# Output weight with 32 rows a partition, in an adaLN decode block with cached attention

## The chip, the cores and the metric

The kernel runs on one core of a Trainium2 chip. The metric is the device time of one execution in microseconds. Five engines work side by side: TensorE (PE) multiplies matrices, VectorE (DVE), ScalarE (ACT) and GpSimd (POOL) do the rest, and SyncE (SP) issues nearly all DMAs. Each core has 16 DMA engines, which move data between the off-chip memory and the on-chip memory of 128 partitions.

## The reference

One decode step (one new token a row) of a block with adaptive layer norm, batch of 4, width D = 512, 32 heads of 128, a cache of 4096 keys and values, and an MLP of width 1792. Everything is float32.

```python
mod = (_silu(c) @ w_mod).reshape(4, 6, 1, -1)
sa, ca, ga, sb, cb, gb = (mod[:, i] for i in range(6))
h = _layernorm(x) * (1 + ca) + sa
q = heads(h @ wq)                                   # 4, 32, 1, 128
p = softmax(einsum("bhqd,bhkd->bhqk", q, k_cache) * 128 ** -0.5)
o = einsum("bhqk,bhkd->bhqd", p, v_cache)           # 4, 32, 1, 128
x = x + ga * (rows(o) @ wo)                         # wo: 4096 x 512
h = _layernorm(x) * (1 + cb) + sb
x = x + gb * (_silu(h @ w1) @ w2)                   # w1: 512 x 1792, w2: 1792 x 512
```

The keys and values are 268 MB each, the weights wq and wo 8.4 MB each, w_mod 6.3 MB, w1 and w2 3.7 MB each.

## The kernel before, in words

A small planner (`Plan`) records every operation with the memory that it reads and writes, and from that derives the semaphore waits; each engine runs its operations in the order in which they are written. TensorE, VectorE and ScalarE run most tiles in a hardware loop.

Attention is cut into N = 32 tiles. A tile is one batch row b and four heads (group t of NT = 8), 8 MB of keys and 8 MB of values; a partition holds 128 keys of one head, a run of 64 KB. `tile(n)` multiplies the keys by the query, VectorE the first 48 of a partition's 128 and GpSimd the rest, sums over the head's width on VectorE, and makes the exponentials; `values(n)` multiplies them with the values on TensorE, normalizes, and writes four columns of `oz` (128 partitions are the head's width, a column is one head of one batch row). Tiles are counted with the batch row innermost: `t, b = divmod(n, B)`. `qw` holds the spread queries, which `qexpand(t)` writes for four batch rows at a time, `qview(n)` reads for a tile, and `qload(n)` copies into a PSUM bank.

Three big buffers of 64 KB a partition hold the stream: A and B take the keys of odd and even tiles, C takes the values. SyncE issues all loads in the order of the program through the one helper `dma` (L249 in the profile), and waits before each until its buffer is free: w_mod, wq, k0, v0, k1, and so on. After tile 30 B is free, and the output weight `wot` goes there, in four pieces behind the last values (`fetch(wot, wov, "o", 0, 4, 6, 7, 8)`). A is free after tile 31's keys; w1 (three pieces) and w2 (five pieces) go there.

In the output weight a partition holds, for each of the eight head groups t, four consecutive rows of wo, 8 KB:

```python
wov = wo.rearrange("(t p r) n -> p t r n", p=P, r=JJ)   # JJ = 4
```

`regroup()` brings the attention's output into that layout: 16 small TensorE matmuls against columns of the identity put `oz` into PSUM, two ScalarE copies bring it to `oz2`. Then 32 matmuls with 512 columns, spread over four column groups of the array, sum into `accw`. `fold` copies `accw` on ScalarE and adds its four groups with four matmuls into `accp`. From there on: gate and residual (`x1`), layer norm, transpose (`h2T`), w1's matmuls half by half (four pieces k of the contraction for the one half, its activation, then the other half), w2's matmuls as its pieces land (ten wide, a fold, then narrow ones straight into `pf`), gate and residual, and the store.

Matmuls are recorded by one helper line (L263), VectorE's two-operand operations by L272 and L276, ScalarE's by L295. A float32 matmul shows as two passes in the trace.

## Time and profile before

| | |
|---|---|
| median of 3 runs | 1319.59 us (1319.52 to 1319.98) |
| the profiled execution's own time | 1319.41 us |
| its span in the trace | 1318.0 us |
| bytes moved | 567.41 MB, 431 GB/s over the span |
| busy: TensorE, VectorE, ScalarE, GpSimd | 399.6, 884.4, 84.8, 710.9 us |
| SyncE's DMA queue (q1), share of 16 engines | 99.6% |

The span runs from the first instruction to the last; the profiled execution's time has 1.4 us more around it. Busy times of engines overlap. In rows of DMAs a packet is one piece of work of one DMA engine: here a contiguous run of data, or the 4 bytes with which an engine reports that its part of a DMA is complete. In the chain of waits each step leads back to what released it. In the timeline a row has the start, the duration, the engine, the line, the operation and its tiles (out<-in), the count, and in brackets the idle time before it with what ended it.

### The profile page before, as it was taken

To read this page: it belongs to the slowest core of one execution; us is meant where nothing else is said; L and a number is where in the kernel's file an instruction comes from. 1 tells how busy PE (TensorE), PEld (TensorE's weight loads), DVE (VectorE), ACT (ScalarE), POOL (GpSimd) and SP (SyncE) were. 2 spreads that over 40 slices of the span, in tenths; PEclk is the share of its full clock that TensorE was granted. 3 is DMA by queue.
4 is the path that set the end of the run, shared out by engine and by line. 5 is a ranking of instruction groups with operands and counts; after the bars stand their busy time and mean duration, and the time that the engine had idled before them with its cause. 6 is when DMAs were issued, how large, how long until landed. Compare 5 with 4: busy or idle time off the path is not lost.

```text
span 1318.0 us, 7633 instructions
## 1 busy us (share of the span) xinstructions
PE 399.6 (30%) x2748; PEld 115.5 (9%) x2748; DVE 884.4 (67%) x585; ACT 84.8 (6%) x288; POOL 710.9 (54%) x104
## 2 busy tenths in 40 slices
PE   2533222333321233322133332113333212333336
PEld 0100000000000000000000000000000000000012
DVE  1367876666876666687666678766667776666871
ACT  1200000000000000000000000000000000000001
POOL 0346665444666444566644456654446665445760
PEclk9766656666656666665666666566666556666668
DMA  9999999999999999999999999999999999999998
GB/s 414 437 424 440 432 432 442 422 440 438 424 442 432 432 440 422 442 438 424 440 428 438 438 424 442 436 426 440 426 438 440 424 442 430 432 440 422 430 425 357
DMA packets 12100, 567.41 MB, mean 431 GB/s; under 512 B 1292, under 2 KB 1340, under 8 KB 2108
## 3 DMA queue, kind: packets, MB, share of 16 engines
q1 hardware_dynamic: 12052, 567.29, 99.6%
q8 instruction: 4, 0.07, 0.0%
q14 instruction: 4, 0.03, 0.0%
q10 hardware_dynamic: 40, 0.02, 0.0%
HBM read 567.30 MB, written 0.01 MB: 430 GB/s over the span
## 4 chain that ended last, share of the span: by engine, by line
DMA 60%; DVE 24%; issue 9%; PE 5%; ACT 1%; SPq 1%; POOL 0%; DVEq 0%; ACTq 0%
DMA k<-in_A_k_cache_dram 55%; DVE sc L281 14%; DVE k L272 8%; PE ps L263 5%; DMA wqt<-in_A_wq_dram 3%; DMA w2t<-in_B_w_dram 2%; ACT sc L295 1%; SPq L249 1%; DVE pz L272 1%; DVE rt L516 1%; DVE nm L280 0%; POOL E L272 0%; DVEq L173 0%; DVE o L276 0%; ACT qs L295 0%
## 5 line engine op out<-in xcount | busy, mean ns | idle before, releaser
L272 POOL TENSOR_TENSOR k<-k,qw 128x3072 f32<-128x3072 f32 (+1 forms) x96 | 706.5, 7387 | 515.4 <-DMA k<-in_A_k_cache_dram 515.4
L263 PE MATMUL ps<-v,pz 128*16 128x512 f32 x2048 | 311.3, 751 | 844.4 <-DMA v<-in_A_v_cache_dram 804.3
L281 DVE TENSOR_REDUCE sc<-k 128x24 f32<-128x3072 f32 (+2 forms) x128 | 559.5, 4413 | 1.1
L272 DVE TENSOR_TENSOR k<-k,ps 128x6144 f32<-128x6144 f32 x32 | 209.7, 6555 | 227.5 <-DMA k<-in_A_k_cache_dram 227.3
L263 PEld LDWEIGHTS ps<-v,pz 128*16 128x16 f32 x2048 | 58.2, 114 | 1041.8 <-DMA v<-in_A_v_cache_dram 789.2
L295 ACT ACTIVATE sc<-sc,nm 128x80 f32<-128x80 f32 x64 | 22.3, 348 | 1005.4 <-DVE nm L280 1005.4
L276 DVE SCALAR_TENSOR_TENSOR o<-ps,fr,o 128x512 f32<-128x512 f32 x32 | 24.0, 751 | 53.0 <-PE ps L263 53.0
L272 DVE TENSOR_TENSOR pz<-sc,ps 128x320 f32<-128x320 f32 x64 | 27.0, 421 | 32.5 <-ACT sc L295 32.5
L263 PE MATMUL ps<-sel,o 128*128 128x4 f32 x256 | 33.8, 255 | 31.1 <-DVE o L276 31.1
L263 PEld LDWEIGHTS ps<-sel,o 128*128 128x128 f32 x256 | 31.0, 191 | 61.4 <-DVE o L276 61.4
L555 DVE RECIPROCAL fr<-ps 128x1 f32<-128x1 f32 x32 | 5.4, 168 | 42.5 <-PE ps L263 42.5
L272 POOL TENSOR_TENSOR E<-qs,sel 128x2048 f32<-128x2048 f32 x1 | 3.6, 3637 | 45.7 <-ACT qs L295 45.7
L295 ACT ACTIVATE o<-ps,fr 128x512 f32<-128x512 f32 x32 | 22.0, 687 | 60.7 <-DVE fr L276 60.7
L281 DVE TENSOR_REDUCE sc<-sc 128x1 f32<-128x80 f32 x64 | 14.1, 220 | 2.2
L516 DVE STREAM_TRANSPOSE rt<-sc 128x32 f32<-128x32 f32 x64 | 13.5, 211 | 2.2
L280 DVE TENSOR_REDUCE nm<-rt 128x1 f32<-128x32 f32 x64 | 11.9, 186 | 2.2
L272 DVE TENSOR_TENSOR x<-mod,ps 128x128 f32<-128x128 f32 x1 | 0.3, 286 | 18.4 <-PE ps L263 18.4
L272 DVE TENSOR_TENSOR E<-qs,sel 128x2048 f32<-128x2048 f32 x1 | 2.3, 2293 | 15.2 <-ACT qs L295 15.2
L263 PE MATMUL ps<-wqt,hT 128*32 128x512 f32 x64 | 9.0, 726 | 11.4 <-DMA wqt<-in_A_wq_dram 11.4
L263 PE MATMUL ps<-X,selp 128*128 128x2 f32 x64 | 12.3, 262 | 0.0
L263 PE MATMUL ps<-wmt,csT 128*32 128x256 f32 (+1 forms) x64 | 6.7, 590 | 18.2 <-DMA wmt<-in_w_mod_dram 18.2
L295 ACT ACTIVATION_READ_ACCUMULATOR sc<-sc,nm 128x1 f32 x64 | 11.9, 187 | 0.0
(70 smaller groups left out, 122.0 us busy)
## 6 DMA issues: line engine op xcount, KB each, us to landing
wmt<-in_w_mod_dram SPq DMA_DIRECT2D x1, 6144.0 KB, 17.3
k<-in_A_k_cache_dram SPq DMA_DIRECT2D x1, 5120.0 KB, 39.2
v<-in_A_v_cache_dram SPq DMA_DIRECT2D x1, 5120.0 KB, 24.8
wot<-in_A_wo_dram SPq DMA_DIRECT2D x1, 4096.0 KB, 37.2
k<-in_A_k_cache_dram SPq DMA_DIRECT2D x1, 3072.0 KB, 46.0
v<-in_A_v_cache_dram SPq DMA_DIRECT2D x1, 3072.0 KB, 27.6
wot<-in_A_wo_dram SPq DMA_DIRECT2D x1, 2048.0 KB, 41.7
wot<-in_A_wo_dram SPq DMA_DIRECT2D x2, 1024.0 KB, 43.9
```

Of the source, the lines that this page charges most:

```text
L249: return pl.op(eng, lambda: e.dma_start(dst, src), [], [dst], sem=s)
L263: lambda: nc.tensor.matmul(o, lhsT, rhs, start=start, stop=stop, skip_group_check=True),
L272: return q(lambda: e.tensor_tensor(o, a, b, op=op), [a, b], [o])
L276: return dve(lambda: V.scalar_tensor_tensor(o, a, s, b, op0=op0, op1=op1), reads, [o])
L280: return dve(lambda: V.tensor_reduce(o, a, axis=AX.X, op=op, negate=True), [a], [o])
L281: return dve(lambda: V.tensor_reduce(o, a, axis=AX.X, op=op), [a], [o])
L295: return act(lambda: A.activation(o, a, fn, **kw), reads, writes)
L516: dve(lambda: V.transpose(rt[:, h, :], a), [rm], [rt[:, h, :]])
L555: dve(lambda: V.reciprocal(fr[:, 0:1], fps[:, 0:1]), [fps[:, 0:1]], [fr[:, 0:1]])
```

## The change

The output weight is read with 32 consecutive rows of wo in each partition (64 KB of one head), in pieces of 16, 8, 4 and 4 rows. Its partitions are ordered by the quarter q of the head's width, then by head. Tiles are counted with the head group innermost, so that the columns of `oz` run through the 32 heads of a batch row; one VectorE transpose in blocks of 32 by 32 then puts `oz` into the weight's layout, and ScalarE and VectorE each spread half of it into `oz2`. The last four rows of the weight are multiplied narrowly, straight into `accp`, behind the fold. w1 comes in two pieces, and its last quarter is multiplied for both halves after the first three quarters of both.

```diff
+    QO = P // H
+    RO = Dh // QO
+    CUTO = (0, 16, 24, 28, 32)
...
-    oz = ozf[:, :].rearrange("p (t b i) -> p t b i", t=NT, b=B)
-    oz2 = sb("oz2", JJ, NT, W)
-    qw = sb("qw", NT, B * Dh)
+    oz2 = sb("oz2", RO, W)
+    qw = sb("qw", B, NT, Dh)
...
-    wot = big("B", "wot", NT, JJ, D)
+    wot = big("B", "wot", RO, D)
...
-    wov = wo.rearrange("(t p r) n -> p t r n", p=P, r=JJ)
+    wov = wo.rearrange("(h q r) n -> q h r n", q=QO, r=RO)
...
     def kload(n, *cuts):
-        t, b = divmod(n, B)
+        b, t = divmod(n, NT)
...
     def vload(n, *cuts):
-        t, b = divmod(n, B)
+        b, t = divmod(n, NT)
...
     def qexpand(t):
...
-        actv(qw[:, t, :], ps[:, :], AF.Copy)
+        actv(qw[:, :, t, :], ps[:, :].rearrange("p (b d) -> p b d", d=Dh), AF.Copy)
...
-    fetch(wot, wov, "o", 0, 4, 6, 7, 8)
+    for lo, hi in zip(CUTO, CUTO[1:]):
+        dma(wot[:, lo:hi, :], wov[:, :, lo:hi, :], f"o{lo}")

     def regroup():
-        for h in range(2):
-            ps = bank[(6, 0)[h]][:, :].rearrange("p (r t w) -> p r t w", r=2, t=NT)
-            for r in range(2):
-                for i in range(HP):
-                    mm(
-                        ps[W * i : W * (i + 1), r, :, :], ident[:, 2 * h + r : P : JJ],
-                        bc(oz[:, :, :, i], 3, R), True, True,
-                    )
-            actv(oz2[:, 2 * h : 2 * h + 2, :, :], ps, AF.Copy)
+        dve(lambda: V.transpose(ozt[:, :], ozf[:, :]), [ozf[:, :]], [ozt[:, :]])
+        src = bc(ozt[:, :].rearrange("p (b r) -> p b r", b=B), 3, R)
+        dst = oz2[:, :, :].rearrange("p r (b c) -> p b r c", b=B)
+        actv(dst[:, 0:2], src[:, 0:2], AF.Copy)
+        dve(lambda: V.tensor_copy(dst[:, 2:4], src[:, 2:4]), [src[:, 2:4]], [dst[:, 2:4]])
...
-    fetch(w1t, w1v, "a", 0, 2, 3, 4)
+    fetch(w1t, w1v, "a", 0, 3, 4)
     fetch(w2t, w2v, "b", 0, 7, 10, 12, 13, 14)
     regroup()
-    for i in range(NT * JJ):
-        g, (t, r) = i % G, divmod(i, JJ)
-        mm(accw[W * g : W * (g + 1), :], oz2[:, r, t, :], wot[:, t, r, :], i < G, i >= NT * JJ - G)
-    fold(accp, wide[0], accw, True, True)
+    RW = CUTO[-2]
+    for r in range(RW):
+        g = r % G
+        mm(accw[W * g : W * (g + 1), :], oz2[:, r, :], wot[:, r, :], r < G, r >= RW - G)
+    fold(accp, wide[0], accw, True, False)
+    for r in range(RW, RO):
+        for g in range(G):
+            mm(accp[W * g : W * (g + 1), :P], oz2[:, r, :], wot[:, r, g * P : (g + 1) * P], False, r == RO - 1)
...
-    for h, ph in ((0, bank[2]), (1, bank[6])):
...
+    halves = (bank[2], bank[6])
+    for k0, k1 in ((0, NK - 1), (NK - 1, NK)):
+        for h, ph in enumerate(halves):
+            pv_ = ph[:, :FH].rearrange("p (c i) -> p c i", i=NH)
+            for k in range(k0, k1):
+                for g in range(G):
+                    mm(
+                        pv_[W * g : W * (g + 1)], h2T[:, k, :], wv[:, k, g, :, NH * h : NH * (h + 1)],
+                        k == 0, k == NK - 1,
+                    )
+    for h, ph in enumerate(halves):
         silu2(hid[:, h, :], ph[:, :FH], hs[:, h, :])
         transposed(hidT[:, NH * h : NH * (h + 1), :], hid[:, h, :], NH)
```

## The prediction

> **What bounds the kernel now.** I read the page first: its slices and its table of DMA queues.

> ```profile
> span 1318.0 us, 7633 instructions
> ...
> DMA  9999999999999999999999999999999999999998
> DMA packets 12100, 567.41 MB, mean 431 GB/s; under 512 B 1292, under 2 KB 1340, under 8 KB 2108
> ...
> q1 hardware_dynamic: 12052, 567.29, 99.6%
> ...
> DMA 60%; DVE 24%; issue 9%; PE 5%; ACT 1%; SPq 1%; POOL 0%; DVEq 0%; ACTq 0%
> ```

> q1, SyncE's queue, keeps its 16 engines busy for 99.6% of the span. One engine thus moves 567.29 MB / (0.996 x 1318.0 us x 16) = 27.0 GB/s while busy. VectorE's 24% of the chain lies beside transfers; nothing but a change in the DMA work can move the time much. Second, the DMA view of the steady stretch, of the output weight, and the end of the chain of waits:

> ```profile
> DMA packets 7489, 436.22 MB, mean 434 GB/s; under 512 B 832, under 2 KB 832, under 8 KB 832
> ...
> DMA packets 801, 6.36 MB, mean 424 GB/s; under 512 B 64, under 2 KB 64, under 8 KB 64
> ...
> 1285.32 28.14 DMA w2t<-in_B_w_dram
> 1313.50 1.23 PE ps L263 x32
> 1314.78 0.47 PE ps L263 x8
> ```

> The first line is 205.27 to 1211.54 us (k and v alone: runs of 64 KB, 434 GB/s, 27.1 an engine), the second 1282 to 1297 us (output weight alone: runs of 8 KB, 424 GB/s). At the end the second MLP weight is what everyone waits for: after its last pieces only 1.7 us of matmuls, two small VectorE operations and the store are left. The order of arrival is v31, output weight, w1, w2, each 16 engines wide.

> **How a transfer is spread over the engines.** This decides the case. In the sums each DMA leaves small completion packets, so they can be counted. SyncE issues 80 loads (wm, wq, 33 k, 33 v, 4 wo, 3 w1, 5 w2). With three small DMAs (c, x, out) left over, 80 x 16 + 3 x 4 = 1292 is exactly the count of packets under 512 B above. So a load whose DRAM side starts with the 128 partitions posts 16 completions, and those three post 4. The three have in common that their DRAM side is written `(g) b d`, with an outer axis of 4. The store alone (1317.1 to 1317.5 us), and the load of c beside the first weight (5.9 to 7.7, then 7.7 to 9.5 us), show it:

> ```profile
> DMA packets 20, 0.01 MB, mean 21 GB/s; under 512 B 4, under 2 KB 20, under 8 KB 20
> ...
> q1 hardware_dynamic: 20, 0.01, 7.5%
> ...
> q1 hardware_dynamic: 16, 0.79, 100.9%
> q10 hardware_dynamic: 4, 0.00, 0.4%
> ...
> q1 hardware_dynamic: 16, 0.79, 100.8%
> q10 hardware_dynamic: 4, 0.00, 0.4%
> ```

> The store has 16 rows and 4 completions. c has 16 rows too, and in each stretch in which all 16 engines take one 48 KB packet of the weight (1.8 us), only 4 of c's rows go: four engines alternate between the queues, one row each a round, and twelve have no row of c at all. Completions and rows agree: an outer axis of 4 puts the whole DMA on 4 engines.

> [...]

> **The change, part by part.**

> *Output weight's load.* Before, `wov` is `p t r n`, outer axis 128, and 16 engines. After, it is `q h r n` with q = 4: sizes 4 and 128, four engines for all four pieces (8 KB loads with 4 and 16 are what the rows show; for 4 and 128 it is taken over). 8.389 MB / 4 = 2.097 MB an engine. The rate of an engine lies between 424 / 16 = 26.5 GB/s (8 KB runs) and 434 / 16 = 27.1 (64 KB runs). The new runs are 32, 16 and 8 KB, half of the bytes in 32, so I take 27.0, the page's mean: 77.7 us (77.4 to 79.1). What the load takes now is read from TensorE's waits, which end as each piece lands:

> ```profile
> 1287.54 3.64 PE L263 MATMUL ps<-wot,oz 128*32 128x512 f32 x32 [0.82 <-DMA wot<-in_A_wo_dram]
> 1292.41 1.92 PE L263 MATMUL ps<-wot,oz 128*32 128x512 f32 x16 [1.24 <-DMA wot<-in_A_wo_dram]
> 1294.90 1.07 PE L263 MATMUL ps<-wot,oz 128*32 128x512 f32 x8 [0.57 <-DMA wot<-in_A_wo_dram]
> 1297.39 1.73 PE L263 MATMUL ps<-wot,oz 128*32 128x512 f32 x8 [1.42 <-DMA wot<-in_A_wo_dram]
> ```

> The last three pieces (4.194 MB) take 1297.39 - 1287.54 = 9.85 us, 426 GB/s, so the whole takes 19.7 us. Difference 77.7 - 19.7 = +58.0 us (57.5 to 59.5). Nothing covers it. w1 and w2 go over 16 engines, and the four loaded ones must still carry their sixteenth of both behind the output weight, in order; the other twelve finish early and stand idle for about 58 us. The time from the last wo byte to the last w2 byte stays what it is, since those four engines still carry 0.459 MB each there (17 us at 27.0). The longer runs alone, on 16 engines, would be worth 19.7 us less 8.389 MB / 434 GB/s = 19.3: -0.4 us.

> *SyncE's queue.* The issues stop when an engine's ring is full:

> ```profile
> 1250.23 12.35 SPq L249 DMA_DIRECT2D wot<-in_A_wo_dram  x4
> ...
> 1280.31 11.45 SPq L249 DMA_DIRECT2D w2t<-in_B_w_dram  x5
> ...
> q1 hardware_dynamic: 9580, 546.28, 100.0%
> ```

> The last line is the DMA view from 0 to 1262.58 us, when wo's fourth issue ends: 9580 / 16 = 599 packets an engine are out. Issued are 68 loads of 9 (8 rows and a completion) and wo's 33 + 17 + 9 + 9: 680. So about 81 packets wait in each ring when an issue is let through. After, each wo piece puts 32 + 1 packets on four engines, 132 in all. The third and fourth issue, and w1 and w2 behind them in SyncE's order, are held until those rings drain to some 80. That holds back twelve empty engines, but not the four that set the end: with 40 to 80 packets waiting they don't run dry. Priced 0; upper bound a dry gap before the later three pieces and before w1, each as long as the store takes from issue to its first packet (1315.91 to 1317.2 us, 1.3): 4 x 1.3 = +5.

> ```profile
> 1315.91 0.69 SPq L664 DMA_DIRECT2D out_dram<-y  x1
> ```

> *w1 in two pieces.* One load of 9 packets an engine fewer, its bytes unchanged: 0, bound by the issue itself, held back less than 2.5 us (11.45 / 5) and covered by the full rings.

> *Tiles by batch row first.* Each tile stays one block of 8 MB read in 64 KB runs; only the order of the blocks changes. SyncE's issues of k for tiles 6, 7 and 8:

> ```profile
> 243.97 0.43 SPq L249 DMA_DIRECT2D k<-in_A_k_cache_dram  x1
> ...
> 282.68 0.44 SPq L249 DMA_DIRECT2D k<-in_A_k_cache_dram  x1
> ...
> 321.38 0.43 SPq L249 DMA_DIRECT2D k<-in_A_k_cache_dram  x1
> ```

> From tile 6 to 7 the next block is one batch row away, from 7 to 8 it goes back to row 0 of the next heads; the distances are 38.71 and 38.70 us. Two different jumps, one price: 0, bounds -0.3 and +0.3 (0.01 us a tile over 32). The scattered write of `qw` is eight ScalarE copies before the stream, of the same number of elements.

> *Regroup.* Out go 16 matmuls (two passes each) and two copies; in come a VectorE transpose (0.40 us for 128x128) and half a copy each on ScalarE and VectorE.

> ```profile
> 1283.48 3.24 PE L263 MATMUL ps<-oz,ident 128*32 128x256 f32 x32 [0.26 <-ACT oz L564]
> ...
> 1286.77 0.60 ACT L295 ACTIVATE oz<-ps 128x512 f32<-128x512 f32 x1 [1.11 <-PE ps L263]
> ...
> 1304.33 0.40 DVE L418 STREAM_TRANSPOSE h2T<-hg 128x128 f32<-128x128 f32 x1
> ```

> It takes 1287.37 - 1283.48 = 3.9 us now and about 1.1 after (0.40 + 0.60 and a handover), -2.8. But it is waited for by wo's matmuls alone, and their first piece will land some 39 us after v31 instead of 10: covered, 0.

> *wo's matmuls and the first fold.* Now eight wide passes, a copy and the fold stand between wo's last byte and x1; after it 32 narrow passes (w2's 16 narrow take 0.87, so 1.7).

> ```profile
> 1299.16 0.60 ACT L295 ACTIVATE wide<-ps 128x512 f32<-128x512 f32 x1 [11.79 <-PE ps L263]
> ...
> 1300.53 0.29 DVE L272 TENSOR_TENSOR x<-mod,ps 128x128 f32<-128x128 f32 x1 [18.43 <-PE ps L263]
> ...
> 1304.79 4.77 PE L263 MATMUL ps<-w1t,h2T 128*32 128x224 f32 x64 [1.37 <-DVE h2T L418]
> ...
> 1308.07 0.36 ACT L295 ACTIVATE hs<-ps 128x224 f32<-128x224 f32 x1 [3.06 <-PE ps L263]
> ...
> 1314.33 0.87 PE L263 MATMUL ps<-w2t,hidT 128*32 128x128 f32 x16
> ```

> 1300.53 - 1297.39 = 3.1 us becomes 1.8, -1.3 on the way to w1's matmuls. Those then reorder (three quarters of both halves, then the rest), which makes half 0's activation wait for nearly all of them: of 4.77 us, half 0 was out after 1308.07 - 1304.79 = 3.3 and is out after 56 of 64 passes, 4.2, +0.9. Both lie ahead of w2's wide matmuls, and w2's landing (1313.50) ends the wait today; taken as 0, bounds -0.5 (only the matmuls after the landing can shrink) and +2 if w2's wide matmuls now end after it.

> **Sum.** Against the profiled execution's own 1319.41 us: 1319.4 + 58.0 = 1377.4 us. The median of the runs, 1319.59, is 0.2 above it, which I leave out.

> **The rivals.**

> *It is not slower: 16 engines after all.* Place: the split of `wov`'s pieces. If the 128 partitions of the SBUF side decide, or a long run is cut further, all engines share and the load takes 19.3 us: 1319.4 - 0.4 = 1319.0, no change. Extra time goes with 8.389 MB / 27.0 x (1/k - 1/16): +58 at k = 4, +19 at k = 8, 0 at 16, so it decides only at k = 16. For it: no row has a large load with a narrow outer axis. Against: c's destination has 16 partitions, enough for 16 engines, and got 4. Chance 0.06.

> *Four engines go faster when twelve are idle.* If 434 GB/s were the limit of something shared, an engine might reach twice its 27: 38.8 us, +19.1, 1338.5 us. Against: the store's 20 packets, with nothing beside them, take 7.5% of 16 x 0.4 us = 0.48 us, and c's four rows beside a full load 0.4% of 16 x 1.8 us = 0.115 us; 16 such rows are 0.46. A packet is not quicker in an empty machine. Those are 512 B packets, though. Chance 0.05. [...]

> *The rings run dry.* The 5 us above: 1382.4 us. Against: some 80 packets wait at each issue. Chance 0.05.

> **How the numbers follow.** My forecast, four engines at their present rate, has 0.84: 1374 to 1380 from the bounds of its terms. The dry rings are added on top (1382.4 and the tail's +2 give 1385). Below, the unproved rate of an engine with idle neighbours is the open term; 10% of the 58 us is -6. I give 1371 to 1386, which leaves out 16 engines, the doubled rate and a little of the forecast's own. What a measurement of this kernel can tell from no change is about 0.2%, 2.6 us: slower 0.94, same 0.05 (16 engines), faster 0.01.

> **What would show it.** In the profile after: packets under 512 B fall by 4 x 12 for wo and by 16 for the w1 piece, to 1228; the DMA row falls to a quarter near the end, with about 108 GB/s for some 58 us; wo's four pieces land about 39, 19, 10 and 10 us apart; SyncE's third and fourth wo issues are held for tens of us; the steady stretch stays at 434 GB/s. It is wrong if the DMA row stays at 9 to the end, if wo's completions count 16, or if four engines move clearly more than 108 GB/s.

## The result, and the profile after

The changed kernel takes 1431.38 us (median of 6 runs, 1427.71 to 1437.96), the kernel before 1319.62 (1319.5 to 1320.8): a ratio of 1.0849, 95% interval 1.082 to 1.0877. The forecast was 1377.4 with a range of 1371 to 1386. Slower was right and the place was right, but the loss is 112 us and not 58. The profiled execution took 1429.46 us.

The page of the changed kernel, slices and DMA queue:

```profile
span 1428.1 us, 7617 instructions
...
DMA  9999999999999999999999999999999999972553
GB/s 412 436 439 422 435 437 439 426 431 437 439 430 430 437 435 437 424 437 435 439 422 437 437 439 420 437 439 437 422 437 437 437 424 435 428 327 61 111 153 99
DMA packets 11397, 567.42 MB, mean 397 GB/s; under 512 B 1228, under 2 KB 1276, under 8 KB 1916
...
q1 hardware_dynamic: 11348, 567.29, 93.7%
```

Packets under 512 B are 1228, the number forecast for four engines a wo piece: 4 completions each instead of 16. Thirty-five slices are as busy as before; all of the loss lies in the last five. The DMA view from 205.27 to 1211.54 us (the same line as before) and a table by stretch show both sides of that border (the last two columns are the busy share of the 16 DMA engines and the rate):

```profile
DMA packets 7489, 436.22 MB, mean 434 GB/s; under 512 B 832, under 2 KB 832, under 8 KB 832
...
core 0: us, PE busy (x) PEld busy (x) DVE busy (x) ACT busy (x) POOL busy (x), PEclk, DMA share, GB/s
1280.00:1330.00 50.00, 2.38 (x24) 1.09 (x12) 1.49 (x3) 1.40 (x3) 0.00 (x0) 0.56 0.25 61
1356.00:1377.00 21.00, 3.98 (x28) 0.95 (x20) 0.00 (x0) 0.00 (x0) 0.00 (x0) 0.66 0.25 98
1380.00:1395.00 15.00, 1.79 (x12) 0.06 (x4) 0.00 (x0) 0.00 (x0) 0.00 (x0) 0.61 1.01 228
```

From 1280 to 1330 us a quarter of the engines is busy, so four, all the time, but they move 61 GB/s, 15 an engine and not 27. From 1356 to 1377 us the same four come to 98. From 1380 to 1395 us all sixteen are busy and move 228 GB/s, where the kernel before had 424 over its output weight. So two effects are to be explained: four engines at half rate, and sixteen at half rate. The timeline shows what each piece cost (rows of TensorE begin when a piece lands; those of SyncE show how long an issue was held):

```profile
1251.64 80.36 SPq L252 DMA_DIRECT2D wot<-in_A_wo_dram  x2
...
1283.49 0.31 DVE L590 STREAM_TRANSPOSE ozt<-oz 128x128 f32<-128x128 f32 x1 [1.35 <-ACT oz L564]
...
1284.50 0.43 DVE L594 COPY oz<-ozt 128x512 f32<-128x512 f32 x1 [0.70 <-ACT oz L298]
1332.06 45.63 SPq L252 DMA_DIRECT2D w1t<-in_B_w_dram  x2
1354.60 5.38 PE L266 MATMUL ps<-wot,oz 128*32 128x512 f32 x32 [71.36 <-DMA wot<-in_A_wo_dram]
1377.73 20.44 SPq L252 DMA_DIRECT2D w2t<-in_B_w_dram  x5
1378.15 3.64 PE L266 MATMUL ps<-wot,oz 128*32 128x512 f32 x16 [18.17 <-DMA wot<-in_A_wo_dram]
1395.17 1.93 PE L266 MATMUL ps<-wot,oz 128*32 128x512 f32 x8 [13.37 <-DMA wot<-in_A_wo_dram]
...
1406.78 1.93 PE L266 MATMUL ps<-wot,oz 128*32 128x128 f32 x32 [8.30 <-DMA wot<-in_A_wo_dram]
1408.77 0.29 DVE L275 TENSOR_TENSOR x<-mod,ps 128x128 f32<-128x128 f32 x1 [123.85 <-PE ps L266]
```

The output weight starts where it did (before: last piece at 1297.39 less 19.7 us, 1277.7). Its four pieces then take 76.9, 23.6, 17.0 and 11.6 us, where four engines at 27 GB/s would take 38.9, 19.4, 9.7 and 9.7. The excess is 38.0 + 4.2 + 7.3 + 1.9 = 51.4 us. From the last piece to the end of the span it is 21.3 us, before 20.6. 1377.4 + 51.4 + 0.7 = 1429.5: the sum closes.

Both effects are in the first piece. w1 is issued at 1332.06 us, and the DMA view of 1277 to 1427 us (40 slices of 3.75 us) shows sixteen engines nearly all busy from its 16th to its 19th slice (1333 to 1348 us), at 121 to 221 GB/s:

```profile
DMA  3122221222222239799222222229999952222100
GB/s 66 44 70 52 70 52 52 70 61 61 52 61 70 70 84 221 121 167 165 58 87 83 92 105 96 105 103 249 248 216 223 216 158 107 108 105 94 60 37 5
```

Until w1's issue, 54.4 us at 61 GB/s bring 3.32 of the piece's 4.19 MB. The rest would take 14.3 us at that rate and took 22.5. So an estimate is that some 8 us of the first piece's 38.0 are of the mixture with w1 and some 30 of the four engines alone. The packet records of the trace agree: a 32 KB packet of the weight took 2.15 us on the mean until 1332 us, and 3.2 us from 1334 to 1351 us.

### The profile page after: what moved, and what is told of

The parts are those of the page before. It is cut to its first block, busy times and chain, and to the rows that moved or that the text cites. A ratio compares the mean times of both kernels' runs of the same rounds, so it can differ in the third digit from the quotient of the medians.

```text
span 1428.1 us, 7617 instructions
## 1 busy us (share of the span) xinstructions
PE 403.9 (28%) x2740; PEld 116.2 (8%) x2740; DVE 884.8 (62%) x587; ACT 84.2 (6%) x287; POOL 710.9 (50%) x104
## 2 busy tenths in 40 slices
DMA packets 11397, 567.42 MB, mean 397 GB/s; under 512 B 1228, under 2 KB 1276, under 8 KB 1916
## 3 DMA queue, kind: packets, MB, share of 16 engines
q1 hardware_dynamic: 11348, 567.29, 93.7%
## 4 chain that ended last, share of the span: by engine, by line
DMA 53%; DVE 22%; SPq 10%; issue 8%; PE 5%; ACT 1%; POOL 0%; another core or an unknown queue 0%; DVEq 0%; ACTq 0%
DMA k<-in_A_k_cache_dram 49%; DVE sc L284 13%; SPq L252 10%; DVE k L275 7%; PE ps L266 5%; DMA wqt<-in_A_wq_dram 3%; DMA w2t<-in_B_w_dram 2%; ACT sc L298 1%; DVE pz L275 0%; DVE rt L518 0%; DVE nm L283 0%; POOL E L275 0%; DVEq L173 0%; ACT qs L298 0%
## 5 line engine op out<-in xcount | busy, mean ns | idle before, releaser
L266 PE MATMUL ps<-wot,oz 128*32 128x512 f32 (+1 forms) x88 | 12.9, 744 | 111.2 <-DMA wot<-in_A_wo_dram 111.2
L518 DVE STREAM_TRANSPOSE rt<-sc 128x32 f32<-128x32 f32 x64 | 13.5, 212 | 2.2
L266 PEld LDWEIGHTS ps<-wot,oz 128*32 128x32 f32 x88 | 3.6, 156 | 118.9 <-issue 75.8
```

Of the source, the lines that this page charges most:

```text
L266: lambda: nc.tensor.matmul(o, lhsT, rhs, start=start, stop=stop, skip_group_check=True),
L518: dve(lambda: V.transpose(rt[:, h, :], a), [rm], [rt[:, h, :]])
```

## The experiments

My theory after the result, called *ports*: what counts is where the engines write. The four engines write partitions 32q + h in step, that is, the same h at the same moment, and their 61 GB/s is little more than two engines' 2 x 27.0 = 54: as if engines at work on partitions 32 apart (0 and 32, 64 and 96) shared one way in, a port, in pairs, and each got half, while partitions 8 or 64 apart don't share one. Port is a word for this guess: the runs time loads into different partitions, and none shows what lies behind. In the expectations engines are numbered in the order of the outer axis; no trace shows their numbers. Rivals: reads from DRAM at power-of-two distances collide (256 KB within an engine, 64 KB between engines), or any DMA on four engines is slow by itself. Times below without a number of runs are of one run; the kernel before took 1319.59 to 1319.83 us beside them.

**Sixteen engines again.**

```diff
-    wov = wo.rearrange("(h q r) n -> q h r n", q=QO, r=RO)
+    wov = wo.rearrange("(p r) n -> p r n", r=RO)
...
-        dma(wot[:, lo:hi, :], wov[:, :, lo:hi, :], f"o{lo}")
+        dma(wot[:, lo:hi, :], wov[:, lo:hi, :], f"o{lo}")
```

> The changed kernel with one thing undone: the weight's partitions are read in the order of its rows (128 blocks of 64 KB, outer axis 128), so that its DMAs go over 16 engines again. Everything else of the change stays. The rows land in other partitions than the regrouped values expect, so the output is not the block's. All theories (half-speed engines from shared SBUF write ports, from reads at power-of-two distances in DRAM, or from any DMA on four engines): the four engines are the whole loss, so 1319 us, 1318 to 1321. If regroup, tile order, w1's pieces or the new order of w1's matmuls cost something of their own, it stays above 1322.

Measured: 1319.76 us (median of 10), ratio 1.000, interval 0.999 to 1.001. Table by stretch:

```profile
1280.00:1300.00 20.00, 12.29 (x118) 4.39 (x110) 2.69 (x8) 3.22 (x5) 0.00 (x0) 0.83 1.01 428
```

Everything else in the change (regroup, tile order, w1's pieces and matmul order, longer runs) is together worth nothing that can be measured, either way. The whole 112 us hang on the view of one load: on its outer axis, and with it on the partitions that its engines write.

**Four DMAs a piece, one a quarter.**

```diff
     for lo, hi in zip(CUTO, CUTO[1:]):
-        dma(wot[:, lo:hi, :], wov[:, :, lo:hi, :], f"o{lo}")
+        for q in range(QO):
+            dma(wot[H * q : H * (q + 1), lo:hi, :], wov[q, :, lo:hi, :], f"o{lo}_{q}")
```

> Each piece of the weight as four DMAs, one a quarter of the head's width: 32 partitions from 32 heads, outer axis 32, so 16 engines, two neighbouring partitions each. The layout is that of the change. [...] Theory four engines (only the number of engines counts): 1319 us. Theory DRAM distances (reads 256 and 512 KB apart collide): at least half rate, 1338 us or more.

Measured: 1342.05 us, where the number of engines alone gave 1319. Table by stretch:

```profile
1280.00:1300.00 20.00, 5.59 (x34) 1.93 (x34) 1.81 (x5) 1.49 (x3) 0.00 (x0) 0.64 0.97 202
```

Sixteen engines, busy 97%, at 202 GB/s. The number of engines alone is not it; 32 neighbouring partitions take in data at half rate. That speaks for the partitions that are written, and would also fit DRAM distances. Partitions 32 apart are then not the only ones to clash: no two of one DMA are 32 apart here.

**Four engines, eight partitions apart.**

```diff
+    woh = wo.rearrange("(m a q r) n -> q a m r n", a=4, q=QO, r=RO)
     for lo, hi in zip(CUTO, CUTO[1:]):
-        dma(wot[:, lo:hi, :], wov[:, :, lo:hi, :], f"o{lo}")
+        for q in range(QO):
+            dma(wot[H * q : H * (q + 1), lo:hi, :], woh[q, :, :, lo:hi, :], f"o{lo}_{q}")
```

> Still four engines, but each DMA fills 32 partitions, eight neighbouring ones an engine, so that the four write at any time to partitions 8 apart and not 32 apart. Heads come in the order of their number modulo 4, so weight rows stand in other partitions than the values and the output is not the block's. Reads are 256 KB apart between engines and 1 MB within one. Theory ports: no shared port, 27 GB/s an engine, wo in 78 us: 1377 us, up to 1388 if w1 and w2 still get in the way at the end. Theory DRAM distances: still powers of two, 1425 us or more. Theory four engines are slow by themselves: 1425 us or more. Packets of 32 KB take 1.21 us by the first, 2.4 us by the others.

Measured: 1391.78 us, 4 above the expected band. Table by stretch:

```profile
1280.00:1328.00 48.00, 7.43 (x52) 2.38 (x44) 1.49 (x3) 1.25 (x3) 0.00 (x0) 0.62 0.25 108
1338.00:1360.00 22.00, 3.59 (x24) 0.43 (x16) 0.00 (x0) 1.88 (x2) 0.00 (x0) 0.58 0.99 227
```

The same share of engines as on the changed kernel, 0.25, but 108 GB/s instead of 61: four engines do run at 27 each when the partitions that they write are 8 apart. Four engines are not slow by themselves, and these reads at power-of-two distances are not slow either. The second effect stays: once w1 and w2 come in beside the weight, sixteen busy engines move 227 GB/s.

**Other distances in DRAM.**

```diff
+    wop = wo[0:4000].rearrange("(q y) n -> q y n", q=QO)[:, 0:992, :].rearrange("q (h r) n -> q h r n", r=31)
     for lo, hi in zip(CUTO, CUTO[1:]):
-        dma(wot[:, lo:hi, :], wov[:, :, lo:hi, :], f"o{lo}")
+        cut = 1 if hi == RO else 0
+        dma(wot[:, lo:hi, :], wop[:, :, lo - cut : hi - cut, :], f"o{lo}")
```

> Four engines and the partitions of the change, but other rows of the weight are read: 62 KB apart within an engine and 1.95 MB (1000 rows) apart between engines, no power of two. The output is not the block's. Theory ports: nothing changes, 1430 us, 1422 to 1440. Theory DRAM distances: packets at full rate, 1377 to 1388 us. Theory four engines are slow by themselves: 1430 us.

Measured: 1438.23 us, no better than the changed kernel's 1427.71 to 1437.96. Table by stretch:

```profile
1280.00:1300.00 20.00, 2.37 (x24) 1.09 (x12) 1.49 (x3) 1.40 (x3) 0.00 (x0) 0.64 0.26 59
```

Other addresses to read from change nothing; with the run before, that leaves where the data is written.

**Eight engines, and two.** The outer axis as 8, so that an engine writes 16 neighbouring partitions, and as 2, 64 neighbouring partitions an engine, so that the two write 64 apart:

```diff
-    wov = wo.rearrange("(h q r) n -> q h r n", q=QO, r=RO)
+    wov = wo.rearrange("(i e r) n -> e i r n", e=8, r=RO)   # the other run: e=2
```

> Outer axis 8: eight engines, sixteen neighbouring partitions each, one DMA a piece. Other weight rows stand in the partitions, so the output is not the block's. Theory ports: engines 0 and 2 start at partitions 0 and 32, 1 and 3 at 16 and 48, and so on: eight engines on four ports in step, packets of 32 KB at 2.4 us, 109 GB/s. Twice the engines of the run with four apart would then bring nothing: 77 us for the weight, 1377 to 1395 us. Theory four engines are slow by themselves, or only the number counts: packets at 1.2 us, 39 us, 1339 to 1350 us.

> [...] Other weight rows stand in the partitions, so the output is not the block's. Theory ports: never a shared port, packets of 32 KB at 1.21 us, 54 GB/s: the first piece in 77.7 us, as long as on the changed kernel's four engines (76.8), so half the engines move as much. Whole: 1319.4 + 135.7 = 1455 us, plus some 10 to 15 for the end where w1 and w2 run beside it: 1460 to 1472. Theory four or fewer engines are slow by themselves: the first piece in 150 us, 1590 us or more.

Measured: 1388.52 us with eight and 1468.25 us with two. Timeline with eight, DMA view of 1278 to 1355 us and timeline with two:

```profile
1263.91 39.97 SPq L252 DMA_DIRECT2D w1t<-in_B_w_dram  x2
...
1325.09 5.41 PE L266 MATMUL ps<-wot,oz 128*32 128x512 f32 x32 [35.87 <-DMA wot<-in_A_wo_dram]
```

```profile
DMA packets 133, 4.16 MB, mean 54 GB/s; under 512 B 2, under 2 KB 2, under 8 KB 2
...
q1 hardware_dynamic: 132, 4.15, 12.5%
...
1353.79 5.73 PE L266 MATMUL ps<-wot,oz 128*32 128x512 f32 x32 [70.58 <-DMA wot<-in_A_wo_dram]
```

Two engines, 64 partitions apart, bring the first piece in at 1353.8 us, the changed kernel's four at 1354.6: half the engines, the same time. Before w1 comes in beside the four, their 61 GB/s are little more than the 54 of two. Eight, 16 partitions apart, end 3 us before four that are 8 apart (1388.52 against 1391.78). That run shows less than hoped: its first piece came at 4.194 MB / (1325.09 - 1277.7) us = 89 GB/s, below the 109 of ports alone, with w1 already beside it, so both effects are in it.

**Four engines apart, w1 and w2 held back.** The run with four apart, and

```diff
...
-    fetch(w1t, w1v, "a", 0, 3, 4)
+    dma(w1t[:, 0:3], w1v[:, 0:3], "a0", after=[wot[:, :, :]])
+    dma(w1t[:, 3:4], w1v[:, 3:4], "a3")
```

The helper `dma` gets the argument `after`: memory that must have been written before the issue.

> The run with four engines apart, and SyncE issues w1 (and w2 behind it) only when all of the output weight has landed. That run was 14 us over the 1377 of four engines at full rate, and its packets were at half rate just while w1 and w2 came beside the weight. Theory mixing (transfers of twelve engines beside those of four slow both): all packets at full rate, 77.7 us for the weight, then a gap of 1 to 3 us: 1380 us, 1378 to 1384. If the 14 us have another cause, 1391 us or more, since the wait adds a gap.

Measured: 1382.68 us. Timeline, and behind it the row of the last piece without the wait:

```profile
1315.62 6.07 PE L266 MATMUL ps<-wot,oz 128*32 128x512 f32 x32 [32.51 <-DMA wot<-in_A_wo_dram]
1335.12 3.64 PE L266 MATMUL ps<-wot,oz 128*32 128x512 f32 x16 [13.43 <-DMA wot<-in_A_wo_dram]
1344.98 1.94 PE L266 MATMUL ps<-wot,oz 128*32 128x512 f32 x8 [6.22 <-DMA wot<-in_A_wo_dram]
...
1354.79 0.82 SPq L252 DMA_DIRECT2D w1t<-in_B_w_dram  x2
...
1354.84 1.93 PE L266 MATMUL ps<-wot,oz 128*32 128x128 f32 x32 [6.56 <-DMA wot<-in_A_wo_dram]
```

```profile
1369.31 1.93 PE L266 MATMUL ps<-wot,oz 128*32 128x128 f32 x32 [12.01 <-DMA wot<-in_A_wo_dram]
```

The later pieces land 19.5, 9.9 and 9.9 us apart, 27 GB/s an engine to the end; without the wait the last came at 1369.31. So the 14 us over 1377 were the mixing. The wait made the kernel 9 us faster; the other 5 go into the gap behind it, since w1 is issued only at 1354.8.

**An extra load on partitions 0 to 15, and on 64 to 79.** The edit is the kernel before, and 1 MB more between wo and w1, which nobody reads, on four engines, each into four neighbouring partitions:

```diff
+    extra = wo[0:2048].rearrange("(i e r) n -> e i r n", e=4, r=NJ)
+    dma(vt[0:16, :, :], extra[:, :, 0 : NJ // 4, :], "e")    # the second run: vt[64:80]
     fetch(w1t, w1v, "a", 0, 2, 3, 4)
...
```

The third run takes e=2 and writes 262 KB an engine to `vt[64:72]`. It is to tell a loss that grows with the number of engines in the extra load from one that takes all sixteen at once. The end waits for the load in all three. That nothing is shared on partitions 0 to 15 was my assumption; no trace shows which engine writes which partitions in the loads beside it.

> [...] 262 KB an engine, 9.7 us at 27 GB/s, while the other twelve engines load w1 and w2. Theory ports: nothing shared, all packets at full rate, 1319.6 + 9.7 = 1329 us, 1327 to 1332. If any load of four engines beside one of sixteen halves both: 1337 us or more.

> [...] Theory clogging (one busy port holds up engines that do not use it): all sixteen at half rate, some 220 GB/s, as in the runs with the weight on four engines; about the same end, 1338 us, since engines 0 to 3 set it. No theory: 1329 as in the run before.

> [...] Theory clogging as seen with four: in the mixed stretch all sixteen still fall to half, some 210 to 230 GB/s. [...] The end says nothing here, 1339 us in both, since engines 0 and 1 set it (9.7 us of extra data at half rate, then their w1 and w2).

Measured: 1328.57, 1339.53 and 1338.01 us. Table by stretch of the three, in that order:

```profile
1300.00:1312.00 12.00, 2.02 (x16) 1.43 (x20) 2.35 (x10) 2.04 (x3) 0.00 (x0) 0.58 1.00 414
...
1300.00:1312.00 12.00, 1.85 (x14) 1.20 (x12) 2.62 (x10) 3.43 (x4) 0.00 (x0) 0.50 1.03 214
...
1300.00:1312.00 12.00, 2.20 (x16) 1.20 (x12) 2.61 (x10) 3.42 (x4) 0.00 (x0) 0.50 1.00 217
```

The three differ in the partitions that the extra load writes, and the third also in its engines. On partitions 0 to 15 the mixture runs at 414 GB/s and costs its 9 us; mixing as such is harmless. On partitions 64 to 79 all sixteen engines fall to half: 214 GB/s, where four engines at half rate and twelve at 27 GB/s would have 12 x 27 + 4 x 13.5 = 378. With only two engines, on partitions 64 to 71, it is still 217, where two at half rate and fourteen at 27 would have 14 x 27 + 2 x 13.5 = 405. The packet records of these traces show that this is no mean of fast and slow engines: of w1's and w2's 14 KB packets that start from 1300 to 1312 us, each of the 47 in the third run took 1.07 to 1.18 us, where each of the 130 in the first took 0.54 to 0.55. (For some 1.5 us around 1305 us w1's 7 KB packets ran at the full rate, 0.29 us.) An extra load of two engines thus slows all sixteen; by what path is not shown. In the changed kernel the four engines fill all 128 partitions, 64 to 79 among them, while w1 comes in beside them.

## Why the prediction was wrong

- **Four engines for the whole load**: right. 1228 small packets, a quarter of the engines busy, and 1319.76 us when the outer axis is 128 again.
- **The rate of an engine**: the step that failed. The term "2.097 MB at 27.0 GB/s = 77.7 us" took the rate from loads in which 16 engines fill all 128 partitions (424 and 434 GB/s), and its bounds (26.5 to 27.1) came from the same loads. Four engines in step on partitions 32 apart have 61 GB/s together in the first 50 us. The load took 129.1 us instead of 77.7; of the 51.4 us too little, some 30 are of the four engines alone (the estimate above). I had asked only whether idle neighbours would make an engine faster; the argument against that (a packet is not quicker in an empty machine) was sound, and none of it bounds the rate from below.
- **SyncE's queue**: the holding was as forecast (the third and fourth issue took 80.36 us). Each came through with some 72 earlier packets an engine waiting, at 1270.14 us 678 - 605.6 and at 1332.0 us, of wo's on the four engines, 99 - 26.5; before, wo's fourth did at 671 - 598.8. No run shows the holding itself to cost anything. What failed beside it is the step "the other twelve finish early and stand idle for about 58 us": it lets w1 and w2 run past the four engines at no cost, a term put at nothing without a reason. They came in while the four still wrote the weight, and the mixture slowed all sixteen. Of the excess, the third and fourth piece's 7.3 and 1.9 us are of that time, and by the estimate some 8 us of the first piece's. Issuing w1 and w2 later, behind the weight, made the run with four engines apart faster and not slower. The upper bound, dry rings, named a cost that didn't occur and missed the one that did.
- **w1's pieces, tile order, regroup, first fold**: 0 each, and right in sum (1319.76 us with 16 engines). The steady stretch stays at 434 GB/s. Regroup takes 1284.93 - 1283.49 = 1.4 us (said: 1.1), all under the load; from the last piece to x1 it is 2.0 us (said: 1.8).
- **The time behind the last wo byte**: said to stay, 21.3 us against 20.6.
- **The rivals**: none came. Each one that left four engines kept them at 27 GB/s or more, so the range ended at 1386 and missed by 45 us.

## What to carry to other kernels

Look at the outer axis of a load's DRAM side before its run length: here 128 made it 16 engines wide (busy share 1.01), 4 made it 4 (0.25) and 2 made it 2 (12.5%), and runs up to four times as long lost 112 us where the same runs on 16 engines gained nothing. Count also which partitions the engines write at the same moment: here engines 32 partitions apart fell to about half rate (61 GB/s for four, 108 at 8 apart), and so did the whole core's transfers beside an extra load of two engines into partitions 64 to 71 (217 GB/s). When busy DMA engines show half the usual rate, vary the destination partitions and the source addresses separately, and see which one moves the rate.
